# Unit stores moved on SyncE's queue, and three of fourteen low-part subtractions of a change of expert moved from VectorE to GpSimd

## The chip, the cores and the metric

The kernel runs on one core of a Trainium2 chip, alone. The metric is the device time of one execution in microseconds (us). The core's engines each work through a queue of their own, in order: TensorE (PE in the profile; its weight loads are PEld), VectorE (DVE), ScalarE (ACT), GpSimd (POOL) and SyncE (SP), which here only issues DMA transfers. They wait for each other on semaphores.

## The reference

Attention with a sigmoid instead of a softmax, then a mixture of experts in which each token goes to one of eight experts, then a gated layer. Everything is float32, apart from the last layer's weights, which come as float64.

```python
scores = scale * np.matmul(q, k.transpose(0, 1, 3, 2)) - np.log(S)      # q, k, v: 4 x 12 x 448 x 64
x = np.matmul(1.0 / (1.0 + np.exp(-scores)), v)                         # to 1792 tokens x 768
...
expert_idx = np.argmax(xn @ en.T / tau, axis=1)                         # one expert of 8 for each token
for e in range(E):
    h = np.maximum(x[mask] @ w1[e], 0.0)                                # w1: 768 x 1024
    out[mask] = gate_w[mask, None] * (h @ w2[e])                        # w2: 1024 x 768
...
return (out @ w_a * (out @ w_b)) @ w_out                                # 768 x 1536, 1536 x 768
```

## The kernel before

**Split products.** TensorE multiplies in a short form of float32 (fp32r in the rows). To keep the reference's precision each operand is split into a high part, a cast on ScalarE, and a low part, the operand minus its high part, a subtraction on VectorE. `split` (L787 the cast, L788 the subtraction) does both. Three products, high by high, low by high and high by low, are added up in PSUM.

**Attention** (0 to about 215 us) runs over 24 pairs of heads, `for i in range(NPR + 1)`. An iteration transposes the q and k of pair i+1, loads q and k of pair i+3 and v of pair i+2 (`load`, on SyncE's queue: q at L538, k at L531 and L533, v at L523 and L525), computes the scores of pair i with their sigmoids on ScalarE (L579, L584), and multiplies the sigmoids of pair i-1 by v (L601), with a turn back to token order two pairs behind (`x_tok`, copied out by VectorE at L617). `pump` runs pieces of the routing in between.

**Units.** In the background the float64 weights of the gated layer are turned into float32 in *units* of 128 x 384 numbers. `prep_load` brings one into `raw` (L182, L186, four buffers); VectorE cuts bits into `m` (L199, L201, two buffers); ScalarE converts the lower words (L203) and makes an absolute value in `ab` (L205, three buffers); GpSimd adds the two integer parts (L206); VectorE finishes the number in `ab` (`prep_finish`, L216); `prep_store` sends it to DRAM as `wm` (L229). `prep_tick` does these in the order store, finish, load, next unit; so `prep_store` sends what an earlier tick has finished.

**Mixture of experts** (210 to 540 us). Tokens are gathered by expert in blocks of 128, in two phases. A block transposes the gathered x (L783), splits it (`x_load`: high parts on ScalarE at L831, low parts on VectorE at L841), multiplies by w1 (`p1_half`: L911 to L913 in the first block, L891 after it), transposes the hidden values h (L962), splits them into hT (`h_split`, L970 and on VectorE L973), multiplies by w2 (`p2`, L1012), scales by the gate (`y_whole` or `y_half`, VectorE L1082 and L1090) and scatters the rows to DRAM from GpSimd's queue (L1104). GpSimd's queue also issues the gather of the block after next (`gather`, L812).

**Changes of expert.** When the next block belongs to another expert, that is known only at run time; the instructions of a change stand in branches (`when_new`). SyncE loads w1 and w2 into `r` (`load_w`, L799); then six parts of w1 (128 x 1024 each, kk = 0 to 5) and eight of w2 (128 x 768 each, kk = 0 to 7) are split by `split_w` into w1h, w1l, w2h and w2l. Within block b the order is: w1's kk 0 and 1 and then, after the next x, kk 2 to 5; at the end of the block w2's kk 0 to 3; in the block behind, w2's kk 4 and 5 after its first product with w1, and kk 6 and 7 after the second. The low parts of hT and of x stand between these on VectorE. In this run's trace the subtractions of a change begin at 280, 301, 352, 388, 408 and 463 us: two pairs that follow each other directly, and two single ones.

**First expert.** Its w1 is loaded and split during the last iterations of attention, one part for each step of the list `early_w`, which `first_expert` makes (an empty step and six splits).

**The gated layer** (540 to 1075 us) reads `wm`, splits it and multiplies; the change does not touch it.

What sets the order of the work is the order in which the program is written (the schedule is manual): each engine gets its instructions in that order. In the block behind a change that order is, in the code before:

```python
when_new(lambda: load_new(1), load)
p1(0, lambda: None)
...
if 0 < b < LIVE - 1:
    prep_store()
either(b, y_whole, y_half)
```

Of the kernel before, what the change touches and what calls it, by code (L numbers as in the profile page):

```python
# [9 lines left out]
F32 = mybir.dt.float32  # L10
# [14 lines left out]
def build(ctx: ExitStack, tc: tile.TileContext, q, k, v, emb, tau, w1, w2, wa, wb, wo, out, dbg=None, stop=None):  # L25
# [6 lines left out]
    nc = tc.nc  # L32
# [20 lines left out]
    LIVE = LIVE0 + -(-CAP[1] // P)  # L53
# [438 lines left out]
    def attention():  # L492
# [21 lines left out]
        def load(i, names):  # L514
            if i >= NPR:
                return
            b, hp = pairs[i]
            for nm in names:
                src = dict(q=q, k=k, v=v)[nm]
                sv = src[b, 2 * hp:2 * hp + 2].rearrange("h (p c) d -> p h c d", c=NCH)  # L520
                if nm == "v":
                    t = raw_p.tile([P, 2, NCH, D], F32, tag=nm, name=nm, bufs=4)
                    nc.sync.dma_start(out=t[:, :, :NCH - 1, :], in_=src[b, 2 * hp:2 * hp + 2, :KC].rearrange(  # L523
                        "h (p c) d -> p h (c d)", c=NCH - 1))
                    nc.sync.dma_start(out=t[half_of(i), :, NCH - 1, :],  # L525
                                      in_=src[b, 2 * hp:2 * hp + 2, KC:].rearrange("h p d -> p h d"))
                elif nm == "k":
                    t = raw_p.tile([P, NCH, 2, D], F32, tag=nm, name=nm, bufs=3)
                    dma = nc.scalar if i < 2 else nc.sync
                    for j in range(2):  # L530
                        dma.dma_start(out=t[:, :NCH - 1, j, :], in_=src[b, 2 * hp + j, :KC].rearrange(  # L531
                            "(p c) d -> p c d", c=NCH - 1))
                    nc.sync.dma_start(out=t[half_of(i), NCH - 1], in_=src[b, 2 * hp:2 * hp + 2, KC:].rearrange(  # L533
                        "h p d -> p h d"))
                else:
                    t = raw_p.tile([CP, NCH, 2, D], F32, tag=nm, name=nm, bufs=3)
                    for j in range(2):
                        nc.sync.dma_start(out=t[:, :, j, :], in_=sv[:, j])  # L538
                raw[i, nm] = t

        def tr_pair(i):

            if i == 1:
                pt = [p() for p in av_ps]
                parts = [(pt[s][:, :S], slice(s, s + 1)) for s in range(2)]
            else:
                both = ps_t.tile([P, 2, 512], F32, tag="pt", name="pt")
                pt = [both[:, s] for s in range(2)]
                parts = [(both[:, :, :S], slice(0, 2))]
            for s, nm in enumerate(("q", "k")):  # L550
                t = raw.pop((i, nm))
                for c in range(NCH):
                    cs, r = (slice(c * CP, (c + 1) * CP), slice(0, CP)) if nm == "q" else key_chunk(i, c)
                    nc.tensor.transpose(out=pt[s][:, cs], in_=t[r, c].rearrange("p h d -> p (h d)"), identity=ident[r, r])
            hi = qk_p.tile([P, 2, S], F32R, tag="qkh", name="qkh")
            lo = qk_p.tile([P, 2, S], F32R, tag="qkl", name="qkl")
            for src, ss in parts:
                h, l = (t[:, ss, :] if src.ndim == 3 else t[:, ss.start, :] for t in (hi, lo))
                nc.scalar.copy(out=h, in_=src)
                nc.vector.tensor_tensor(out=l, in0=src, in1=h.bitcast(F32), op=ALU.subtract)  # L560
            QK[i] = (hi, lo)
# [83 lines left out]
        for i in range(NPR + 1):  # L645
            if 0 < i and i + 1 < NPR:
                tr_pair(i + 1)
            load(i + 3, "qk")
            load(i + 2, "v")
            if i < NPR:  # L650
                score_half(i, 0)
            misc["ps"] = av_ps[i % 2]
            if i == NPR:
                one, turn = misc["ps"], [0]

                def either():
                    turn[0] ^= 1
                    return ps_s.tile([P, 2, 512], F32, tag="ps", name="pm2")[:, 0] if turn[0] else one()

                misc["ps"] = either  # L660
            pump((True,))
            if early_w is None and misc.get("flags0"):
                early_w = first_expert()
            if misc.get("tables0") and not misc.get("gathered"):
                gather(0)
                misc["gathered"] = True
            if early_w:
                early_w.pop(0)()
            if 1 <= i <= NPR:
                av_part(i - 1, 0)  # L670
            pump((True,))
            if i < NPR:
                score_half(i, 1)
            pump((LATE,))
            if i % 2 and i >= 2:
                x_tok(i - 2)
            if 1 <= i <= NPR:
                av_part(i - 1, 1)
            if i == NPR:
                both = ps_s.tile([P, 2, 512], F32, tag="ps", name="px0")  # L680
                x_load(0, [both[:, hf] for hf in range(2)])
                gather(1)
            if i >= 2:
                if i % 2 == 0:
                    x_tok(i - 2)
                b, hp = pairs[i - 2]
                if hp == NP - 1:
                    routed(b)
            if i < 3:
                prep_load(i)  # L690
            elif i < NPR:
                prep_tick(nc.sync)
                if i % 6 == 3 and i > 3:
                    prep_tick(nc.sync, 1)
            pump((END,))
# [101 lines left out]
    def load_w(which, expert, pair):  # L797
        t, src = (r1[pair], w1) if which == 1 else (r2[0][:, 2 * pair:2 * pair + 2, :], w2)
        nc.sync.dma_start(out=t, in_=src[expert, 2 * pair * P:2 * (pair + 1) * P, :].rearrange("(k p) c -> p k c", p=P))  # L799

    def split_w(which, kk, pool=None):
        hi, lo = (w1h, w1l) if which == 1 else (w2_t["h"], w2_t["l"])
        t = r1[kk // 2][:, kk % 2, :] if which == 1 else r2[0][:, kk, :]
        split(hi[kk], lo[kk], t, hi[kk].bitcast(F32))

    def gather(b):
        if b >= NBLK:
# [173 lines left out]
    def moe(r2_p):  # L981
# [8 lines left out]
        def block1(b, chg, was_new, load, e_load, live):  # L990
# [47 lines left out]

            if b > 0:
                when_new(lambda: load_new(1), load)  # L1040
                p1(0, lambda: None)
                when_new(lambda: split_new(2, KF // 2, KF - 2), was_new)
                tick()

                def rest():
                    when_new(lambda: split_new(2, KF - 2, KF), was_new)

                p1(1, rest)
                tick()
                if b < LIVE - 1:  # L1050
                    prep_tick()
                when_new(lambda: load_new(2), load)
# [37 lines left out]
                    nc.vector.scalar_tensor_tensor(out=yo[:PH], in0=yp[hf][PH:, :HD], scalar=gt[:PH], in1=yo[:PH],  # L1090
                                                   op0=ALU.mult, op1=ALU.add)

            if 0 < b < LIVE - 1:
                prep_store()
            either(b, y_whole, y_half)
            if live is not None:
                tc.mark_branch_hint_location(f"live{b + 1}", live, [ET.Activation, ET.DVE])
# [8 lines left out]

        for i in range(2, KF // 2):
            load_w(2, e_of[0], i)

        def block(b, was_new=None):  # L1110
            nx = b + 1
# [253 lines left out]
```

## Time and profile before

| | |
|---|---|
| time, median of 3 runs | 1075.32 us (1074.67 to 1077.29) |
| profiled execution: its own time | 1076.83 us |
| profiled execution: span from first to last instruction | 1074.9 us |
| mean granted clock of TensorE, as a share of its higher level | 0.997 |
| TensorE busy | 1049.5 us, 98% |
| VectorE busy | 592.3 us, 55% |
| ScalarE busy | 510.4 us, 47% |
| GpSimd busy | 154.2 us, 14% |
| TensorE's largest wait, for the first q at the start | 6.0 us |

The profile is of one execution; its own time is 1.5 us above the median of the runs. Busy shares are means over three stages that differ: VectorE is busy for 97% of the stretch from 280 to 320 us, and for 46% of the gated layer (246.8 of 535 us). A line of the timeline gives an instruction's start, its duration, the engine, the code's line and operation, the tile that it writes and those that it reads. Several equal instructions in a row stand on one line (x4) with the time from the start of the first to the end of the last.

### The profile page before, as it was taken

How to read it: one execution, taken by the hardware profiler on the slowest of the kernel's cores; microseconds unless marked ns; L12 is line 12 of the kernel's file. 1: busy time of each engine (PE TensorE's matmuls, PEld its weight loads, DVE VectorE, ACT ScalarE, POOL GpSimd, SP SyncE). 2: the span in 40 equal slices, each digit the busy share in tenths (PEclk: the TensorE clock that was granted, in tenths of full speed). 3: DMA queues.
4: the chain of work that ended last, by engine and by line, in shares of the span. 5: the costliest groups of instructions: out<-in, count | busy, mean ns of one | idle time of the engine just before them, and what ended most of it. 6: DMA issues, size and time to landing. Idle time of an engine off the chain costs nothing. (4 is left out here: it accounts for less than half of the span.)

```text
span 1074.9 us, 17443 instructions
## 1 busy us (share of the span) xinstructions
PE 1049.5 (98%) x5916; PEld 848.5 (79%) x5916; DVE 592.3 (55%) x1061; ACT 510.4 (47%) x803; POOL 154.2 (14%) x222
## 2 busy tenths in 40 slices
PE   7999999999999999999999999999999999999998
PEld 4554555488878977998978888888888888888997
DVE  2566698868793869372256786333333333333553
ACT  5777676543673777262155554333323322332542
POOL 2031221423222222221102222000000000000000
PEclk9999999999999999999999999999999999999999
DMA  6687769648589778822184644292220272210820
GB/s 161 170 207 200 186 175 260 197 146 292 174 307 331 253 262 305 317 86 101 47 279 176 221 132 145 105 361 109 88 88 1 107 289 89 89 45 1 350 105 30
DMA packets 118051, 187.84 MB, mean 175 GB/s; under 512 B 53928, under 2 KB 89000, under 8 KB 113072
## 3 DMA queue, kind: packets, MB, share of 16 engines
q1 hardware_dynamic: 113296, 171.10, 47.5%
q0 software_dynamic: 3040, 14.94, 3.9%
q8 instruction: 56, 0.92, 0.3%
q10 hardware_dynamic: 1600, 0.39, 0.2%
q14 instruction: 59, 0.48, 0.1%
HBM read 154.17 MB, written 32.24 MB: 173 GB/s over the span
## 5 line engine op out<-in xcount | busy, mean ns | idle before, releaser
L1229 PE MATMUL ab<-yh,whi 128*128 128x512 f32 (+1 forms) x576 | 209.3, 363 | 0.4 <-DVE yl L788 0.4
L1230 PE MATMUL ab<-yl,whi 128*128 128x512 f32 (+1 forms) x576 | 209.3, 363 | 0.2 <-DVE yl L788 0.2
L1231 PE MATMUL ab<-yh,wlo 128*128 128x512 f32 (+1 forms) x576 | 209.0, 363 | 0.0
L206 POOL TENSOR_TENSOR m<-m,raw 128x384 int32<-128x384 int32 x72 | 75.9, 1054 | 353.8 <-DVE m L201 193.4
L1231 PEld LDWEIGHTS ab<-yh,wlo 128*128 128x128 f32 x576 | 108.8, 189 | 17.3 <-DVE wlo L788 0.3
L1229 PEld LDWEIGHTS ab<-yh,whi 128*128 128x128 f32 x576 | 108.8, 189 | 16.3 <-ACT whi L787 0.5
L1230 PEld LDWEIGHTS ab<-yl,whi 128*128 128x128 f32 x576 | 108.8, 189 | 16.2 <-DVE yl L788 0.9
L1262 PE MATMUL o<-whi,gh 128*128 128x512 f32 x336 | 114.7, 341 | 0.0
L1263 PE MATMUL o<-whi,gl 128*128 128x512 f32 x336 | 113.7, 338 | 0.0
L1264 PE MATMUL o<-wlo,gh 128*128 128x512 f32 x336 | 113.0, 336 | 0.0
L1237 DVE TENSOR_TENSOR m<-ab,a 128x512 f32<-128x512 f32 (+1 forms) x48 | 30.0, 624 | 144.6 <-issue 126.5
L787 ACT CAST gh<-m 128x512 fp32r<-128x512 f32 (+1 forms) x48 | 27.2, 567 | 166.4 <-DVE m L1237 166.4
L584 ACT ACTIVATE a<-ps,bias_s 128x896 f32<-128x896 f32 x96 | 92.9, 1006 | 26.5 <-PE ps L579 25.8
L788 DVE TENSOR_TENSOR wlo<-r,whi 128x768 fp32r<-128x768 f32 x76 | 68.6, 954 | 57.3 <-ACT whi L787 57.3
L787 ACT CAST whi<-r 128x768 fp32r<-128x768 f32 x76 | 58.9, 833 | 54.6 <-PE o L1263 46.0
L601 PE MATMUL av<-a,v 128*64 128x448 f32 (+1 forms) x384 | 79.8, 571 | 2.0 <-DVE xtok L617 2.0
L788 DVE TENSOR_TENSOR wlo<-wx,whi 128x768 fp32r<-128x768 f32 x57 | 51.2, 954 | 44.0 <-ACT whi L787 44.0
L1262 PEld LDWEIGHTS o<-whi,gh 128*128 128x128 f32 x336 | 63.4, 189 | 8.2
L1263 PEld LDWEIGHTS o<-whi,gl 128*128 128x128 f32 x336 | 63.4, 189 | 7.5
L1264 PEld LDWEIGHTS o<-wlo,gh 128*128 128x128 f32 x336 | 63.1, 188 | 7.4
L973 DVE SCALAR_TENSOR_TENSOR hTl<-px,hTh 128x512 fp32r<-128x512 f32 x35 | 24.1, 689 | 73.2 <-ACTq L993 63.7
L787 ACT CAST whi<-wx 128x768 fp32r<-128x768 f32 x57 | 43.8, 832 | 40.7 <-PE o L1263 36.0
(271 smaller groups left out, 1847.6 us busy)
## 6 DMA issues: line engine op xcount, KB each, us to landing
r<-in_moe_w_dram SPq DMA_DIRECT2D x28, 768.0 KB, 14.6
wx<-wm SPq DMA_DIRECT2D x18, 1152.0 KB
r<-wm SPq DMA_DIRECT2D x17, 1152.0 KB, 5.6
r<-in_moe_w_dram SPq DMA_DIRECT2D x18, 1024.0 KB, 10.9
raw<-in_moe_w_a_dram SPq DMA_DIRECT2D x24, 384.0 KB, 3.7
raw<-in_moe_w_b_dram SPq DMA_DIRECT2D x24, 384.0 KB, 3.7
raw<-in_moe_w_out_dram SPq DMA_DIRECT2D x24, 384.0 KB, 3.9
wm<-ab SPq DMA_DIRECT2D x48, 192.0 KB, 2.6
```

The source lines that it names most:

```text
L206: nc.gpsimd.tensor_tensor(out=m, in0=m, in1=low, op=ALU.add)
L584: nc.scalar.activation(out=a[r], in_=ps[:n, :, :S], func=AF.Sigmoid, bias=bias_s[:n], scale=qscale)
L601: nc.tensor.matmul(av[w][j * D:(j + 1) * D, :S], lhsT=raw[w, "v"][r, j, c, :], rhs=a[r, j, :], start=first, stop=last)
L787: nc.scalar.copy(out=hi, in_=src)
L788: eng.tensor_tensor(out=lo, in0=src, in1=f32_hi, op=ALU.subtract)
L1229: nc.tensor.matmul(ps[:, :n], lhsT=hi[:, s, cs], rhs=yh[:, kk, :n], start=kk == 0, stop=False)
L1230: nc.tensor.matmul(ps[:, :n], lhsT=hi[:, s, cs], rhs=yl[:, kk, :n], start=False, stop=False)
L1231: nc.tensor.matmul(ps[:, :n], lhsT=lo[:, s, cs], rhs=yh[:, kk, :n], start=False, stop=kk == KD - 1)
L1237: nc.vector.tensor_tensor(out=m, in0=ps[:, :n], in1=a, op=ALU.mult)
L1262: nc.tensor.matmul(t[:, d0:d1], lhsT=gh[:, cs], rhs=hi[:, 2, d0:d1], start=first, stop=False)
L1263: nc.tensor.matmul(t[:, d0:d1], lhsT=gl[:, cs], rhs=hi[:, 2, d0:d1], start=False, stop=False)
L1264: nc.tensor.matmul(t[:, d0:d1], lhsT=gh[:, cs], rhs=lo[:, 2, d0:d1], start=False, stop=last)
```

## The change

Four edits. In attention, `prep_store` is called ahead of the loads of q, k and v in each iteration, besides its call in `prep_tick`. The step of `early_w` is taken ahead of the lines that make that list, so that each step comes an iteration later, and the last one behind the loop. In the mixture of experts, `prep_store` moves from the place ahead of y's scaling to the place behind w1's loads at the head of the block. And `split_w` gives the subtraction of w1's part kk = 3 and of w2's parts kk = 2 and 5 to GpSimd; this holds at each change of expert, and for w2's part 5 also once in the first block, where the first expert's w2 parts 4 to 7 are split.

```diff
--- before.py
+++ after.py
@@ -645,6 +645,7 @@
         for i in range(NPR + 1):
             if 0 < i and i + 1 < NPR:
                 tr_pair(i + 1)
+            prep_store()
             load(i + 3, "qk")
             load(i + 2, "v")
             if i < NPR:
@@ -658,14 +659,14 @@
                     return ps_s.tile([P, 2, 512], F32, tag="ps", name="pm2")[:, 0] if turn[0] else one()
 
                 misc["ps"] = either
+            if early_w:
+                early_w.pop(0)()
             pump((True,))
             if early_w is None and misc.get("flags0"):
                 early_w = first_expert()
             if misc.get("tables0") and not misc.get("gathered"):
                 gather(0)
                 misc["gathered"] = True
-            if early_w:
-                early_w.pop(0)()
             if 1 <= i <= NPR:
                 av_part(i - 1, 0)
             pump((True,))
@@ -798,10 +799,12 @@
         t, src = (r1[pair], w1) if which == 1 else (r2[0][:, 2 * pair:2 * pair + 2, :], w2)
         nc.sync.dma_start(out=t, in_=src[expert, 2 * pair * P:2 * (pair + 1) * P, :].rearrange("(k p) c -> p k c", p=P))
 
+    on_pool = {}
+
     def split_w(which, kk, pool=None):
         hi, lo = (w1h, w1l) if which == 1 else (w2_t["h"], w2_t["l"])
         t = r1[kk // 2][:, kk % 2, :] if which == 1 else r2[0][:, kk, :]
-        split(hi[kk], lo[kk], t, hi[kk].bitcast(F32))
+        split(hi[kk], lo[kk], t, hi[kk].bitcast(F32), nc.gpsimd if kk in on_pool.get(which, ()) else nc.vector)
 
     def gather(b):
         if b >= NBLK:
@@ -1038,6 +1041,8 @@
 
             if b > 0:
                 when_new(lambda: load_new(1), load)
+                if b < LIVE:
+                    prep_store()
                 p1(0, lambda: None)
                 when_new(lambda: split_new(2, KF // 2, KF - 2), was_new)
                 tick()
@@ -1090,8 +1095,6 @@
                     nc.vector.scalar_tensor_tensor(out=yo[:PH], in0=yp[hf][PH:, :HD], scalar=gt[:PH], in1=yo[:PH],
                                                    op0=ALU.mult, op1=ALU.add)
 
-            if 0 < b < LIVE - 1:
-                prep_store()
             either(b, y_whole, y_half)
             if live is not None:
                 tc.mark_branch_hint_location(f"live{b + 1}", live, [ET.Activation, ET.DVE])
@@ -1106,6 +1109,8 @@
 
         for i in range(2, KF // 2):
             load_w(2, e_of[0], i)
+
+        on_pool.update({1: (3,), 2: (2, 5)})
 
         def block(b, was_new=None):
             nx = b + 1
```

Lines of the code behind the first edit move: the subtraction of L788 is L789 in the changed kernel, the gather of L812 is L815, y's scatter of L1104 is L1107.

SyncE's queue in attention, in the iteration that starts near 93 us: q, k, v and raw are loads into SBUF tiles of those names, wm is the store of a finished unit. Before:

```order
L186 DMA raw<-in_moe_w_out_dram 128x768
L538 DMA q<-in_q_dram 112x4x64 x2
L531 DMA k<-in_k_dram 128x3x64 x2
L533 DMA k<-in_k_dram 64x2x64
L523 DMA v<-in_v_dram 128x2x192
L525 DMA v<-in_v_dram 64x2x64
L229 DMA wm_69<-ab 128x384 x2
L182 DMA raw<-in_moe_w_a_dram 128x3x256
```

In the changed kernel:

```order
L186 DMA raw<-in_moe_w_out_dram 128x768
L229 DMA wm_69<-ab 128x384 x2
L538 DMA q<-in_q_dram 112x4x64 x2
L531 DMA k<-in_k_dram 128x3x64 x2
L533 DMA k<-in_k_dram 64x2x64
L523 DMA v<-in_v_dram 128x2x192
L525 DMA v<-in_v_dram 64x2x64
L182 DMA raw<-in_moe_w_a_dram 128x3x256
```

The two stores stand ahead of the five lines of loads instead of behind them.

GpSimd's queue in a block of the mixture of experts, from x's transposes to y's scatter; xg is the gathered x, m a unit's integer part, the branches are those of `when_new` and of the block's other conditions. Before:

```order
L823 UNCONDITIONAL_BRANCH
L993 COMPARE_AND_BRANCH
L993 UNCONDITIONAL_BRANCH x2
L812 DMA xg<-xs,idx_100 128x768
L876 UNCONDITIONAL_BRANCH
L206 TENSOR_TENSOR m<-m,raw 128x384
...
L1104 DMA ys<-y,idy_102 5376x768
```

In the changed kernel, and on to the first branch behind the scatter:

```order
L789 TENSOR_TENSOR w1l_131<-r_1_2831,w1h_125 128x1024
L996 UNCONDITIONAL_BRANCH x3
L815 DMA xg<-xs,idx_100 128x768
L879 UNCONDITIONAL_BRANCH
L206 TENSOR_TENSOR m<-m,raw 128x384
...
L789 TENSOR_TENSOR w2l_2825<-r_2946,w2h_2817 128x768
L996 UNCONDITIONAL_BRANCH x2
L1107 DMA ys<-y,idy_102 5376x768
...
L789 TENSOR_TENSOR w2l_2828<-r_2946,w2h_2820 128x768
```

At a change, w1's part stands ahead of the gather and of the unit's addition, w2's kk 2 between that addition and the scatter, and w2's kk 5 behind the scatter.

VectorE's queue in the same block, the low parts of w1's kk 2 to 5 and what follows. Before:

```order
L788 TENSOR_TENSOR w1l_130<-r_1_2830,w1h_124 128x1024
L788 TENSOR_TENSOR w1l_131<-r_1_2830,w1h_125 128x1024
L788 TENSOR_TENSOR w1l_132<-r_2_2831,w1h_126 128x1024
L788 TENSOR_TENSOR w1l_133<-r_2_2831,w1h_127 128x1024
L993 UNCONDITIONAL_BRANCH x2
L216 SCALAR_TENSOR_TENSOR ab<-ab,m 128x384
```

In the changed kernel:

```order
L789 TENSOR_TENSOR w1l_130<-r_1_2831,w1h_124 128x1024
L789 TENSOR_TENSOR w1l_132<-r_2_2832,w1h_126 128x1024
L789 TENSOR_TENSOR w1l_133<-r_2_2832,w1h_127 128x1024
L996 UNCONDITIONAL_BRANCH x3
L216 SCALAR_TENSOR_TENSOR ab<-ab,m 128x384
```

The second of the four subtractions is gone from this queue; the unit's finish follows the third.

## Rows read from the trace of the kernel before

**Rows 1.** The page's first part: busy time, share of the span, instructions.

```profile
PE 1049.5 (98%) x5916; PEld 848.5 (79%) x5916; DVE 592.3 (55%) x1061; ACT 510.4 (47%) x803; POOL 154.2 (14%) x222
```

**Rows 2.** TensorE's waits: engine, line, releaser: us in total, times, longest us.

```profile
PE av L601 <- DVE xtok L617: 2.0, 2, 1.8
PE ps L579 <- ACT a L584: 1.6, 1, 1.6
```

**Rows 3.** Stretches in attention: us, busy PE, PEld, DVE, ACT, POOL, PEclk, DMA, GB/s.

```profile
100.00:105.00 5.00, 3.40 (x24) 1.83 (x23) 1.93 (x4) 2.81 (x4) 1.01 (x1) 1.00 0.93 262
105.00:110.00 5.00, 4.97 (x27) 2.44 (x24) 1.47 (x3) 3.23 (x5) 0.00 (x0) 0.66 0.79 208
205.00:210.00 5.00, 5.00 (x23) 2.12 (x22) 4.54 (x15) 0.26 (x1) 2.07 (x2) 0.67 0.00 0
```

**Rows 4.** Two stretches of the same view where changes of expert follow each other.

```profile
280.00:300.00 20.00, 20.00 (x113) 18.08 (x111) 19.43 (x26) 18.20 (x28) 5.54 (x4) 1.00 0.53 179
300.00:320.00 20.00, 17.69 (x89) 14.41 (x89) 19.26 (x25) 15.10 (x24) 5.26 (x4) 1.00 0.89 335
```

**Rows 5.** ScalarE's timeline: start us, us, instruction, in brackets idle time before it.

```profile
102.19 0.56 ACT L205 ACTIVATE ab<-raw 128x384 f32<-128x384 bf16 x1 [3.91 <-DMA wm<-ab]
```

**Rows 6.** SyncE's queue on the timeline; last, how long `ab`'s stores took to land.

```profile
93.60 2.57 SPq L538 DMA_DIRECT2D q<-in_q_dram  x2
99.59 1.01 SPq L229 DMA_DIRECT2D wm<-ab  x2
...
DMA to landing us min/median/max: 2.5/3.6/4.7
```

**Rows 7.** VectorE's timeline ahead of those stores.

```profile
92.48 1.02 DVE L216 SCALAR_TENSOR_TENSOR ab<-ab,m 128x384 f32<-128x384 f32 x2
```

**Rows 8.** Timelines of ScalarE and TensorE around the first expert's sixth step.

```profile
203.91 1.04 ACT L787 CAST w1h<-r 128x1024 fp32r<-128x1024 f32 x1
210.84 0.48 ACT L831 CAST xh<-px 128x384 fp32r<-128x384 f32 x1 [0.62 <-DVE xl L860]
...
214.64 0.39 PE L912 MATMUL p<-w1l,xh 128*128 128x512 f32 x1
```

**Rows 9.** VectorE's timeline at the change at 352 us.

```profile
355.98 4.62 DVE L788 TENSOR_TENSOR w1l<-r,w1h 128x1024 fp32r<-128x1024 f32 x4
363.71 5.30 DVE L788 TENSOR_TENSOR w2l<-r,w2h 128x768 fp32r<-128x768 f32 x6
368.93 0.68 DVE L973 SCALAR_TENSOR_TENSOR hTl<-px,hTh 128x512 fp32r<-128x512 f32 x1
```

**Rows 10.** GpSimd's elementwise forms: one line's durations (min/median/max), one group of lines.

```profile
L206 POOL TENSOR_TENSOR m<-m,raw x48: 1009/1021/2062, 38.4 to 449.7; 128x384 int32<-128x384 int32 x48
...
L114 POOL TENSOR_TENSOR fold<-ident 128x64 f32<-128x64 f32 x2 | 0.6, 320 | 0.0
```

**Rows 11.** Timelines of VectorE and GpSimd where their instructions meet.

```profile
300.82 1.83 DVE L788 TENSOR_TENSOR w1l<-r,w1h 128x1024 fp32r<-128x1024 f32 x1
...
300.55 1.02 POOL L206 TENSOR_TENSOR m<-m,raw 128x384 int32<-128x384 int32 x1 [6.91 <-DVE m L201]
...
205.33 1.21 DVE L788 TENSOR_TENSOR w1l<-r,w1h 128x1024 fp32r<-128x1024 f32 x1
...
205.35 2.06 POOL L206 TENSOR_TENSOR m<-m,raw 128x384 int32<-128x384 int32 x1 [5.65 <-ACT w1h L787]
```

**Rows 12.** Timelines of TensorE and GpSimd after the change at 352 us.

```profile
361.13 1.52 PE L891 MATMUL p<-w1l,xh 128*128 128x512 f32 x6
370.49 1.55 PE L1012 MATMUL p<-w2h,hTl 128*128 128x384 f32 x8
...
362.18 1.03 POOL L206 TENSOR_TENSOR m<-m,raw 128x384 int32<-128x384 int32 x1 [6.18 <-DVE m L201]
```

**Rows 13.** Timelines of VectorE and TensorE at the last change.

```profile
477.12 0.68 DVE L973 SCALAR_TENSOR_TENSOR hTl<-px,hTh 128x512 fp32r<-128x512 f32 x1
...
480.79 1.55 PE L1012 MATMUL p<-w2h,hTl 128*128 128x384 f32 x8
```

## The prediction

> **What bounds the kernel now.** The page's first part comes first: TensorE is busy 98% of the span [rows 1], so a change counts by what it takes from, or adds to, TensorE's 25 us of idle time, and by the clock granted to TensorE. Next, the list of what TensorE waited for [rows 2]. Once the first loads are there, two single waits stand out, both in attention: 1.6 us for ScalarE's sigmoids and 1.8 us for a copy of VectorE. Behind each of them the table of stretches shows a granted clock of 0.66 and 0.67 for about 5 us, where it is 1.00 elsewhere [rows 3]: each wait costs its own length and then some 5 x 0.34 = 1.7 us more.
>
> Then the mixture of experts. TensorE hardly waits there, but at a change of expert VectorE is not idle either: where two changes follow each other it is busy 38.7 of 40 us [rows 4]. So the second question is how much VectorE may be late before TensorE notices.
>
> **Stores ahead of q, k, v.** The wait of 1.6 us, just before 105 us, has its origin in ScalarE's queue: from 98.3 us on its activation into `ab` stands still for 3.91 us until a unit's store has landed, and the cast of the next pair's q and k stands behind it [rows 5]. The two stores left at 99.59 us, behind q, k and v that SyncE had begun to issue at 93.60 us [rows 6], although VectorE had finished what they store by 93.5 us [rows 7]. With the stores ahead of q, k, v they leave at about 93.6 us and land within 2.5 to 4.7 us as such stores do [rows 6], at the latest at 98.3 us, when ScalarE asks. The stall goes, and with it TensorE's 1.6 us and the 1.7 us of clock: **-3.3 us**. Bounds: 0, if another wait takes that place, and -6.8 if the second wait (1.8 us and its 1.7 us of clock) goes as well; I count nothing for that one, because in the new order a low part of w1 still stands ahead of that copy on VectorE. That q, k, v leave about 1 us later I cost at nothing: they are issued two pairs ahead of the transposes that read them; the price without that cover would be up to 1 us for each pair.
>
> **First expert's low parts.** Moving the pop ahead of the two lines that make the list shifts all six steps by one iteration; the sixth falls behind the loop, after x's high parts. Its cast starts at 211.3 us, when ScalarE is through with x [rows 8], takes 1.04 us as the fifth part's did [rows 8], and the subtraction 1.15 to 1.21 us [rows 9, 11]: ready at 213.6 us, a microsecond before TensorE reads it at 214.64 [rows 8]. I cost it at nothing; if VectorE's queue delays it by 2 us, it costs 1 us.
>
> **Unit stores behind w1's loads.** SyncE reaches w1's loads without first waiting for VectorE's unit, so they leave some microseconds earlier where two changes follow each other. There ScalarE's casts waited for weights, but VectorE, whose subtractions follow these casts, was busy all along [rows 4]. So I count nothing for it; the most it could return is TensorE's idle time in such a stretch, 20.00 - 17.69 = 2.3 us [rows 4]. In exchange a store now waits until w1's loads have found their buffers free, and `ab` comes back later to ScalarE, whose casts of weights stand behind the activation that waits for it. `ab` has three buffers and a block makes at most two units, so I cost that at nothing; without the cover it would be a stall like the one in attention, 1.6 us of TensorE.
>
> **Three low parts on GpSimd.** This is the term that decides. VectorE gives up one of w1 (4.62 / 4 = 1.15 us) and two of w2 (5.30 / 6 = 0.88 us each) at a change [rows 9]. No row shows GpSimd subtracting weights. Its addition of 384 columns takes 1.02 us and one of 64 columns 0.32 us [rows 10]; the line through both gives 2.42 us for 1024 columns and 1.86 us for 768. Bounds: VectorE's own 1.15 and 0.88 below, and in proportion to the 384 columns above, 2.72 and 2.04.
>
> Does VectorE go on working meanwhile? At 300.82 us a subtraction of w1 takes 1.83 us, where another takes 1.21; GpSimd's addition runs until 301.57, and from there the subtraction needs those 1.1 to 1.2 us [rows 11]. The reverse is there too: at 205.35 us GpSimd's addition takes 2.06 us, because VectorE began such a subtraction 0.02 us earlier [rows 11]. So an elementwise instruction of GpSimd and a subtraction of VectorE from two SBUF tiles run one after the other, not side by side.
>
> The Trainium skill says the same as a rule (SBUF — State Buffer, "Who interferes with whom"): a VectorE instruction with two SBUF inputs and a GpSimd instruction that reads SBUF share a port, and the second to come waits for the whole of the first. It speaks against this change, and the rows above agree; by it the sum is the one below, without it the first rival's.
>
> So each moved part costs VectorE's chain GpSimd's time less its own: 2.42 - 1.15 = 1.27 us for w1, 1.86 - 0.88 = 0.98 us for each of w2. The single change at 352 us shows what TensorE feels. VectorE finishes w1's last low part at 360.60 us; TensorE reads it as the last of six that start at 361.13, at 362.3 [rows 9, 12]: 1.27 us late is still in time. GpSimd's addition for a unit follows this and now ends near 364.5 us instead of 363.21 [rows 12]; w2's 3rd part goes straight behind it, and VectorE's subtractions stand until it is done. The 6th comes behind the scatter of y and stops VectorE once more, before hT's low part. That is ready at 369.61 us now and read at 370.49 [rows 9, 12]: 0.88 us of slack against 1.27 + 2 x 0.98 = 3.23 us. TensorE loses 2.35 us.
>
> There are six changes. Two pairs follow each other directly (the first at 280 and 301 us [rows 4, 11]); with VectorE full, nothing is caught up between the two: 2 x 3.23 - 0.88 = 5.6 us a pair. The one at 352 us costs 2.35. The last has no units beside it: GpSimd's part of w2 falls beside y's scaling, and hT's low part is ready at 477.80 us, 3.0 us before it is read [rows 13], against 3.2 us: nothing. The gather that now stands behind w1's part on GpSimd fetches what is read a block later, some 20 us on where two changes follow each other (280 and 301 us): its 2.4 us cost nothing; without that cover they would come on top at each change. Sum: 2.35 + 2 x 5.6 = **+13.5 us**, in pieces of about 1 us, shorter than the waits behind which the clock fell, so I add nothing for the clock.
>
> By the figure of the Trainium skill (GPSIMD Engine Reference, "3.1 Elementwise — side-by-side cycle accounting": 4497 ns for an addition of 2048 columns) the two sizes would be about 2.25 and 1.69 us, an estimate, and the sum +11 instead of +13.5 us. No run here shows it yet.
>
> **Sum.** -3.3 + 13.5 = +10.2 us. The profiled execution took 1076.83 us, which becomes 1087.0; the median of the runs is 1075.32, 1.5 us lower, so I forecast **1085.5 us**.
>
> **Rivals.** First, the other side: GpSimd's subtraction of fp32 lets VectorE's run beside it, where the integer addition did not. VectorE is then 2.9 us earlier at each change, and TensorE's waits in the two pairs go, 2 x 2.3 us [rows 4]; with attention's 3.3 that is -7.9: 1067.4 us. What decides is whether a subtraction of VectorE beside one of GpSimd keeps its 1.21 us; against it stand the two collisions of [rows 11], for it only that none of them is fp32.
> Second, the instructions do exclude each other, but GpSimd's turns fall mostly where VectorE waits or reads PSUM, or w1's earlier loads move the pairs: a third of 13.5 remains, +4.5 - 3.3 = +1.2: 1076.5 us. Against it: VectorE has 1.3 us free in 40 [rows 4].
> Third, it is dearer: GpSimd needs 2.72 and 2.04 us, 3.89 us a change, so 3.0 + 2 x 6.9 = 16.8; and the waits grow long enough to lower the clock twice, 3.4 us: +20.2 - 3.3 = 1092.2 us; without the clock 1088.8, which is also what comes if attention gives nothing.
>
> **How the numbers follow.** The forecast (1079 to 1088.5) 0.50; the first rival 0.17; the second 0.15; the third 0.18. A measurement of this kernel tells about 0.3% from no change, 1072.1 to 1078.5 us. Faster: the first rival and a little, 0.18. Same: most of the second, 0.14. Slower: 0.68. The range reaches down into the second rival and up to the third, 1074 to 1092, and leaves out the first and the ends.
>
> **What would show it.** Right: GpSimd's three rows at a change near 2.4 and 1.9 us; subtractions of VectorE of 2 to 3.5 us that end 0.9 to 1.2 us after GpSimd's; TensorE waiting for hT's and w2's low parts on VectorE, about 1 us at a time; no wait of ScalarE for a unit's store in attention, and no clock of 0.66 near 105 us. Wrong: VectorE's subtractions all at 1.21 and 0.95 us (the first rival), or stretched ones without new waits of TensorE (the second).

## The result, and the profile after

The changed kernel takes 1087.13 us (median of 6 runs, 1086.57 to 1089.2) where the kernel before takes 1075.68: a ratio of 1.011, 95% interval 1.0098 to 1.0123, or 11.5 us more. The forecast was 1085.5 us. The profiled execution took 1087.26 us, with a span of 1085.5; its span is 10.6 us longer than that of before.

The changed kernel's page, first part, and the list of what TensorE waited for (us in total, times, longest us):

```profile
PE 1052.4 (97%) x5916; PEld 852.1 (78%) x5916; DVE 606.1 (56%) x1042; ACT 510.1 (47%) x803; POOL 188.8 (17%) x241
```

```profile
PE p L1015 <- DVE w2l L789: 6.7, 6, 1.7
...
PE p L894 <- DVE xl L844: 4.7, 2, 2.4
PE p L1015 <- DVEq L996: 3.5, 5, 1.8
PE av L601 <- DVE xtok L617: 1.9, 2, 1.7
```

Against [rows 1]: VectorE made 19 instructions fewer and was busy 13.8 us longer. It didn't get more work; its instructions stood still inside. That is seen in the durations of the changes' subtractions (count, then ns min/median/max), before:

```profile
L788 DVE TENSOR_TENSOR w2l<-r,w2h x48: 944/951/959, 291.8 to 478.6; 128x768 fp32r<-128x768 f32 x48
L788 DVE TENSOR_TENSOR w1l<-r,w1h x36: 1207/1215/1833, 280.6 to 469.7; 128x1024 fp32r<-128x1024 f32 x36
```

In the changed kernel, with GpSimd's own:

```profile
L789 DVE TENSOR_TENSOR w2l<-r,w2h x32: 943/946/2800, 293.9 to 484.9; 128x768 fp32r<-128x768 f32 x32
L789 DVE TENSOR_TENSOR w1l<-r,w1h x30: 1211/1218/3421, 280.3 to 481.2; 128x1024 fp32r<-128x1024 f32 x30
L789 POOL TENSOR_TENSOR w2l<-r,w2h x11: 1840/1847/1868, 291.7 to 482.3; 128x768 fp32r<-128x768 f32 x11
L789 POOL TENSOR_TENSOR w1l<-r,w1h x6: 2396/2582/3030, 284.4 to 477.6; 128x1024 fp32r<-128x1024 f32 x6
```

Against [rows 2]: the wait for ScalarE's sigmoids (L579 on L584, 1.6 us) is gone, the one for `xtok` is still there, and, apart from the wait for the first q, three entries head the list, all of them VectorE's: low parts of w2 and low parts of x, which are new, and, as "DVEq", VectorE's queue that comes late to a branch (1.3 us in 4 waits before).

The table of stretches, for the changed kernel (columns as in [rows 3]):

```profile
100.00:105.00 5.00, 5.00 (x36) 2.36 (x32) 1.83 (x3) 3.96 (x5) 1.02 (x1) 1.00 0.72 202
105.00:110.00 5.00, 5.00 (x40) 3.23 (x39) 4.04 (x8) 4.32 (x6) 1.02 (x1) 1.00 0.89 222
200.00:206.00 6.00, 6.00 (x31) 2.82 (x30) 5.31 (x17) 1.67 (x3) 1.14 (x2) 0.72 0.33 117
238.00:242.00 4.00, 4.00 (x19) 4.00 (x18) 2.40 (x9) 0.75 (x2) 1.01 (x1) 0.57 0.15 53
310.00:314.00 4.00, 4.00 (x12) 3.15 (x11) 3.97 (x7) 0.89 (x2) 0.00 (x0) 0.57 0.29 99
422.00:426.00 4.00, 3.78 (x10) 3.02 (x11) 4.00 (x6) 2.40 (x4) 0.55 (x1) 0.61 0.46 129
```

The clock of 0.66 behind 105 us [rows 3] is 1.00 now. The one behind 200 us has stayed, and three new ones have come, at 238, 310 and 422 us. Each takes about 1.7 us of TensorE's time: 6 x 0.28 for the first, 4 x 0.43 for the second and third; the fourth lasts beyond the end of its stretch.

Where the time went is seen when the same matmul of TensorE is looked up in two traces. In times of the kernel before, 197 to 253 us holds the end of attention and the experts' first block, 275 to 345 the first pair of changes, 345 to 391 the single one, 391 to 454 the second pair. The table gives the lead (-) or lag (+) in us against the trace of before, for the changed kernel and for the experiments below, from one profile each. At 90 us, ahead of the first effect, they lie between -0.4 and +0.1:

| kernel | 105 | 197 | 253 | 275 | 345 | 391 | 454 | end |
|---|---|---|---|---|---|---|---|---|
| changed kernel | -1.8 | -4.1 | -0.7 | -0.3 | +3.5 | +5.6 | +10.5 | +10.6 |
| a_no_pool | -1.6 | -2.5 | -2.4 | -1.6 | -2.7 | -2.7 | -3.4 | -3.3 |
| b_pool_only | -0.6 | -2.2 | +1.0 | +1.1 | +4.9 | +6.9 | +11.8 | +11.9 |
| c_pool_from_change | -1.7 | -3.9 | -2.2 | -1.9 | +3.3 | +6.8 | +13.0 | +13.1 |
| d_pool_short | -2.0 | -4.3 | -4.1 | -3.1 | -6.5 | -6.5 | -9.9 | -9.8 |
| k_first_block_only | -1.7 | -3.9 | -3.1 | -2.7 | -3.8 | -3.9 | -4.5 | -4.2 |
| e_att_store | -1.7 | -3.5 | -4.0 | -4.0 | -4.0 | -4.0 | -4.0 | -4.0 |
| g_moe_store | -0.3 | -1.8 | -1.8 | -1.7 | -3.4 | -3.4 | -4.1 | -4.0 |
| l_two_stores | -2.1 | -3.9 | -4.3 | -3.7 | -4.9 | -4.9 | -5.5 | -5.2 |

In the changed kernel attention gains, the first block gives 3.4 us of it back, the two pairs lose 3.8 and 4.9 us and the single change 2.1; the last change loses nothing.

**The single change**, where [rows 9] and [rows 12] stand for before. GpSimd's, VectorE's and TensorE's timelines of the changed kernel:

```profile
360.38 2.60 POOL L789 TENSOR_TENSOR w1l<-r,w1h 128x1024 fp32r<-128x1024 f32 x1 [5.23 <-ACT w1h L788]
363.13 1.78 POOL L815 DMA_INDIRECT xg<-xs,idx  x1 [0.16 <-PE p L894]
366.76 1.03 POOL L206 TENSOR_TENSOR m<-m,raw 128x384 int32<-128x384 int32 x1 [1.85 <-ACT w2h L788]
367.75 1.84 POOL L789 TENSOR_TENSOR w2l<-r,w2h 128x768 fp32r<-128x768 f32 x1
369.75 1.12 POOL L1107 DMA_INDIRECT ys<-y,idy  x1 [0.16 <-PE p L894]
370.89 1.86 POOL L789 TENSOR_TENSOR w2l<-r,w2h 128x768 fp32r<-128x768 f32 x1
```

```profile
361.29 3.90 DVE L789 TENSOR_TENSOR w1l<-r,w1h 128x1024 fp32r<-128x1024 f32 x2 [0.59 <-ACT w1h L788]
...
366.45 1.14 DVE L1087 TENSOR_SCALAR y<-p,slots 128x384 f32<-128x384 f32 x2
367.83 2.18 DVE L216 SCALAR_TENSOR_TENSOR ab<-ab,m 128x384 f32<-128x384 f32 x1 [0.24 <-POOL m L206]
369.93 5.38 DVE L789 TENSOR_TENSOR w2l<-r,w2h 128x768 fp32r<-128x768 f32 x4
```

```profile
371.39 0.52 PE L1015 MATMUL p<-w2h,hTh 128*128 128x384 f32 x2
373.62 0.62 PE L1015 MATMUL p<-w2l,hTh 128*128 128x384 f32 x2 [1.72 <-DVE w2l L789]
```

To read there: `ab`'s finish on VectorE, 0.51 us in [rows 7], takes 2.18 us at 367.83; GpSimd's w2 part began at 367.75 and ends at 369.59, 0.42 us before it. The four subtractions of w2 take 5.38 us in place of 4 x 0.88: GpSimd's second part runs in the middle of them. TensorE feels that at once, at the low part of w2's second row block, 1.72 us. y's scaling at 366.45, which reads PSUM, lies beside GpSimd's addition (366.76 to 367.79) and takes its usual time (1.14 us for two, as in the kernel before at 311.31 us). On this last point the trace agrees with the Trainium skill (SBUF — State Buffer, "Who interferes with whom"): outside VectorE's two-port modes an instruction with at most one SBUF input doesn't contend with GpSimd.

**The second change of a pair** shows something else. TensorE, VectorE and GpSimd of the changed kernel:

```profile
422.22 2.40 PE L894 MATMUL p<-w1h,xh 128*128 128x512 f32 x6 [2.36 <-DVE xl L844]
```

```profile
416.52 5.18 DVE L789 TENSOR_TENSOR w1l<-r,w1h 128x1024 fp32r<-128x1024 f32 x2
421.62 1.01 DVE L844 TENSOR_TENSOR xl<-px,xh 128x384 fp32r<-128x384 f32 x2
```

```profile
418.22 2.40 POOL L789 TENSOR_TENSOR w1l<-r,w1h 128x1024 fp32r<-128x1024 f32 x1 [0.95 <-ACT w1h L788]
```

In program order w1's kk 3 comes after the next x. But GpSimd's queue is empty and VectorE's is not: GpSimd takes kk 3 at 418.22 us, just ahead of VectorE's kk 1, which then stands until 420.62. Behind it stands x's low part, and for that TensorE waits 2.36 us; the clock falls behind this wait. The same happens in the first pair (2 waits, 4.7 us in the list above).

The fall of the clock adds little to the loss of the first pair, since TensorE, slower for a while, then waits less for VectorE. The changed kernel's next wait of the first pair, and the same wait in b_pool_only, whose clock doesn't fall in that pair:

```profile
320.98 0.62 PE L1015 MATMUL p<-w2l,hTh 128*128 128x384 f32 x2 [0.62 <-DVE w2l L789]
```

```profile
322.36 0.62 PE L1014 MATMUL p<-w2l,hTh 128*128 128x384 f32 x2 [1.71 <-DVE w2l L788]
```

Both kernels lose 3.8 us in the first pair (table).

### The profile page after: what moved, and what is told of

Read it like the earlier page. It is cut to its first block, busy times and chain, and to the rows that moved or that the text cites. A ratio compares the mean times of both kernels' runs of the same rounds, so it can differ in the third digit from the quotient of the medians.

```text
span 1085.5 us, 17566 instructions
## 1 busy us (share of the span) xinstructions
PE 1052.4 (97%) x5916; PEld 852.1 (78%) x5916; DVE 606.1 (56%) x1042; ACT 510.1 (47%) x803; POOL 188.8 (17%) x241
## 4 chain that ended last, share of the span: by engine, by line
PE 52%; DVE 1%; issue 0%; ACT 0%; POOL 0%; ACTq 0%; POOLq 0%
PE ab L1235 11%; PE ab L1236 11%; PE ab L1234 11%; PE o L1267 6%; PE o L1268 5%; PE o L1269 5%; PE p L1015 2%; PE p L894 2%; PE ab L784 0%; DVE yl L789 0%; PE px L965 0%; PE px L784 0%; DVE wlo L789 0%; PE px L963 0%; DVE y L1087 0%
## 5 line engine op out<-in xcount | busy, mean ns | idle before, releaser
L584 ACT ACTIVATE a<-ps,bias_s 128x896 f32<-128x896 f32 x96 | 92.8, 1005 | 32.4 <-PE ps L579 31.8
L788 ACT CAST gh<-m 128x512 fp32r<-128x512 f32 (+1 forms) x48 | 27.2, 567 | 167.2 <-DVE m L1242 167.2
L789 DVE TENSOR_TENSOR wlo<-r,whi 128x768 fp32r<-128x768 f32 x76 | 68.6, 955 | 57.1 <-ACT whi L788 57.1
L788 ACT CAST whi<-r 128x768 fp32r<-128x768 f32 x76 | 59.0, 833 | 54.3 <-PE o L1268 46.1
L789 DVE TENSOR_TENSOR wlo<-wx,whi 128x768 fp32r<-128x768 f32 x57 | 51.2, 954 | 43.3 <-ACT whi L788 43.3
L1015 PE MATMUL p<-w2h,hTl 128*128 128x384 f32 x288 | 60.1, 343 | 3.5 <-DVEq L996 3.5
```

The lines of the kernel that those rows point to most:

```text
L584: nc.scalar.activation(out=a[r], in_=ps[:n, :, :S], func=AF.Sigmoid, bias=bias_s[:n], scale=qscale)
L788: nc.scalar.copy(out=hi, in_=src)
L789: eng.tensor_tensor(out=lo, in0=src, in1=f32_hi, op=ALU.subtract)
L1015: nc.tensor.matmul(yp[hf][:, :HD], lhsT=l[:, kk, :], rhs=wv[kk][:, hf * HD:(hf + 1) * HD], start=kk == 0 and i == 0 and len(parts) == 2, s ...
```

## The experiments

Each was timed beside the kernel before; ratios are to that, with 95% intervals. One per cent is 10.8 us.

**a_no_pool.** The changed kernel without GpSimd's parts:

```diff
-        on_pool.update({1: (3,), 2: (2, 5)})
```

> The changed kernel without the three parts on GpSimd: only the stores and the first expert's steps are moved. My theory (the loss is GpSimd's three subtractions, which keep VectorE waiting, and the moved stores gain in attention alone): 1075.7 - 4 = 1071.7 us; the -4 is what the changed kernel had gained by 201 us, 4.4 us, less the 0.44 us by which its first load came earlier. Rival one (the stores behind w1's loads cost or gain in the experts, too): off by over 1.5 us from that, and the difference arises between 280 and 430 us. Rival two (the loss comes from the moved stores and not from GpSimd): near 1083 to 1087 us.

1072.05 us, ratio 0.9962 (0.9947 to 0.9977). The loss is GpSimd's parts: 1.011 - 0.9962 makes 15.9 us. The time is within 0.4 us of my theory's. But the gain is not attention's alone: part of it arises in the pairs (table: -1.1 and -0.7 us), so rival one is right about the place, not about the size.

**b_pool_only.** The kernel before, with those lines of the diff alone that hold `on_pool`:

```diff
+    on_pool = {}
...
+        split(hi[kk], lo[kk], t, hi[kk].bitcast(F32), nc.gpsimd if kk in on_pool.get(which, ()) else nc.vector)
...
+        on_pool.update({1: (3,), 2: (2, 5)})
```

> The kernel before with the three parts on GpSimd and nothing else. My theory: the changed kernel lost 4.2 us in the first block, 3.9 and 5.2 us in the two pairs of changes and 1.9 us in the single one, all through GpSimd, and 0 in the last; so 1075.7 + 15.2 = 1090.9 us, and in attention the two waits of the kernel before are still there. Rival (the earlier loads of w1 brought the changes of expert closer and added to the loss): the pairs cost clearly less than 9.1 us, 1086 us or below; or, if the earlier loads had helped, more than 1093 us.

1090.21 us, ratio 1.0145 (1.0123 to 1.0167), +15.6 us. By the table 3.2 us arise from 197 to 253 us, 3.8 and 4.9 in the pairs, 2.0 in the single change: the changed kernel's pattern, with no help from the stores.

**c_pool_from_change.** The first block's part goes back to VectorE:

```diff
                 split_new(2, 4, KF)
+                on_pool.update({1: (3,), 2: (2, 5)})
...
-        on_pool.update({1: (3,), 2: (2, 5)})
```

> The changed kernel, but the first block's w2 part 5 goes back to VectorE; the changes of expert stay as they are. My theory (that one part delays the gather and the routing's small operations behind it on GpSimd by 1.7 us, TensorE waits 1.8 us for hT's low part and then loses about as much by the lower clock): 1087.1 - 4 = 1083.1 us, with no wait of TensorE near 237 us and a clock of 1.00 from 238 to 242 us. Rival (the first block's wait has to do with its shifted first expert's steps or with the stores, not with this part): 1086 to 1088 us, the wait still there.

1089.73 us, ratio 1.013 (1.0109 to 1.015): not faster. The wait near 237 us is gone, but 1.7 us are lost from 197 to 253 us all the same, because the low clock behind 200 us lasts twice as long here (0.50 from 204 to 206 us, where the changed kernel has 0.90). And the table shows that the changes cost more: 5.2, 3.5 and 6.2 us in place of 3.8, 2.1 and 4.9. For the single change the reason is seen on TensorE's timeline of this kernel, at the place shown above for the changed one:

```profile
371.21 0.51 PE L1015 MATMUL p<-w2h,hTh 128*128 128x384 f32 x2
373.45 0.62 PE L1015 MATMUL p<-w2l,hTh 128*128 128x384 f32 x2 [1.72 <-DVE w2l L789]
373.90 0.87 PE L965 MATMUL px<-ident,h 128*128 128x128 f32 x4
374.42 0.99 PE L1015 MATMUL p<-w2h,hTh 128*128 128x384 f32 x2
```

In the changed kernel the two lines that follow the same wait of 1.72 us read:

```profile
374.08 0.60 PE L965 MATMUL px<-ident,h 128*128 128x128 f32 x4
374.43 0.60 PE L1015 MATMUL p<-w2h,hTh 128*128 128x384 f32 x2
```

Same instructions, same wait, but 0.99 us for two matmuls in place of 0.60: here the clock fell (0.57 from 374 to 378 us), there it did not (1.00). That is 1.4 us (3.5 - 2.1). In the pairs the clock falls once in either kernel, but here at the last wait of the pair (1.73 us, until 319.4, and 1.74 us, until 435.7), with no later wait to take up the loss. So the time of such a kernel depends on which of its waits the clock falls behind, and a wait removed early in the kernel can be outweighed by that. My expectation failed, and this run doesn't say what the first block costs.

**d_pool_short.** As c, with shorter subtractions on GpSimd:

```diff
+        if kk in on_pool.get(which, ()):
+            cs = slice(0, 64)
+            nc.scalar.copy(out=hi[kk], in_=t)
+            nc.gpsimd.tensor_tensor(out=lo[kk][:, cs], in0=t[:, cs], in1=hi[kk].bitcast(F32)[:, cs], op=ALU.subtract)
...
```

> As the kernel before this one, but each of GpSimd's three subtractions at a change takes 64 columns instead of 1024 or 768, so most of these three low parts is left out; queues, waits and VectorE's relief are the same. My theory (the price is the time for which GpSimd's instruction keeps VectorE's from starting): VectorE gives up 2.9 us at each change and stands for some 0.3 us three times, so the pairs lose nothing and gain up to 2.3 us each: 1067 to 1072 us. Rival (the price is the new waits and branches in the queues, GpSimd's starting late or the gather behind it, not the length of its instructions): above 1077 us.

1067.71 us, ratio 0.9921 (0.9906 to 0.9937): 22 us less than c, with the same queues and waits. The length of GpSimd's instructions is the price. Against a_no_pool it is 4.4 us less: that is what VectorE's relief is worth in itself, and by the table it arises in the pairs (3.4 us gained in each, in place of 1.1 and 0.7). In the stretch of the first pair this kernel has no wait at all and VectorE is free for 5.3 us (columns as in [rows 4]):

```profile
280.00:320.00 40.00, 40.00 (x217) 36.22 (x216) 34.69 (x50) 32.17 (x52) 14.89 (x16) 1.00 0.78 271
```

**j_unread.** As c, but TensorE does not read GpSimd's results:

```diff
+            run_over(xh, w1l[:3] + w1l[2:3] + w1l[4:], last=True)
...
+                            wk = wv[kk - 1 if b and wv is w2l and kk in (2, 5) else kk]
```

> As the run in which GpSimd has its three parts from the first change of expert on, and GpSimd writes them in full, but TensorE reads the neighbouring low parts in their place from the second block on, so the product leaves these three low parts out and counts their neighbours' twice: no instruction of TensorE waits for GpSimd's results. My theory (GpSimd's instructions keep VectorE's from starting): the time stays where it was, 1087 to 1091 us, and VectorE's subtractions of 2.8 us are all there. Rival (TensorE waits for GpSimd's own late results): near 1070 us.

1085.72 us, ratio 1.0093 (1.008 to 1.0107), a little below the range that I gave. Nothing of TensorE waits for GpSimd here, yet 14.1 us of c's 18.1 (both against a_no_pool) are there. VectorE's subtractions as grouped for that run (ns min/median/max):

```profile
L789 DVE TENSOR_TENSOR w2l<-r,w2h x34: 941/947/2789, 291.2 to 483.9; 128x768 fp32r<-128x768 f32 x34
L789 DVE TENSOR_TENSOR w1l<-r,w1h x30: 1210/1218/3431, 277.6 to 478.5; 128x1024 fp32r<-128x1024 f32 x30
```

The stretched ones are there, up to 2.79 and 3.43 us. The remaining 4 us fit the clock: c's profile has two falls more among the changes (three against one), and its low clock behind 200 us lasts twice as long; that is read from two profiles, not shown.

**k_first_block_only.** The kernel a with the first block's part alone on GpSimd:

```diff
+        on_pool.update({2: (5,)})
...
                 split_new(2, 4, KF)
+                on_pool.clear()
```

> The run without GpSimd's parts (1072.1 us), but with the first block's w2 part 5 on GpSimd, and none at the changes. My theory (this one part delays the gather and the routing's small operations on GpSimd by 1.7 us; TensorE waits 1.8 us near 237 us and loses 1.7 us by the clock): 1075.5 us. Rival (it costs nothing by itself, as the run in which it alone was taken back did not become faster): 1072 us, without the wait.

1073.91 us, ratio 0.9975 (0.9965 to 0.9985), 1.4 us above a_no_pool, with intervals that overlap: between my theory and the rival. In the profile TensorE waits 0.84 us at 236.4 us, without a fall of the clock; in the changed kernel it is 1.79 us, with one. GpSimd's queue shows a reason. The changed kernel's timeline, then this one's:

```profile
222.51 1.88 POOL L789 TENSOR_TENSOR w2l<-r,w2h 128x768 fp32r<-128x768 f32 x1 [15.59 <-PE p L1015]
225.25 1.67 POOL L815 DMA_INDIRECT xg<-xs,idx  x1 [0.86 <-POOLq L996]
```

```profile
222.52 1.90 POOL L789 TENSOR_TENSOR w2l<-r,w2h 128x768 fp32r<-128x768 f32 x1 [15.48 <-ACT w2h L788]
224.56 1.51 POOL L815 DMA_INDIRECT xg<-xs,idx  x1
```

In the changed kernel GpSimd stands 0.86 us at the branch around w1's part (L996), and the gather starts 0.69 us later. Behind the gather stand the routing's small operations of phase 2, then VectorE's chain that turns them into y and hT's low part, and TensorE at its end. That the later gather makes up the whole difference of the two waits (0.95 us) fits, but is not shown by a run of its own.

**e_att_store, f_early_w, g_moe_store, l_two_stores.** Each is the kernel before with some of the other hunks of the diff: the first alone, the second alone, the moved store of the experts alone, and the first with the moved store. As an example, what l changes:

```diff
+            prep_store()
             load(i + 3, "qk")
...
                 when_new(lambda: load_new(1), load)
+                if b < LIVE:
+                    prep_store()
...
-            if 0 < b < LIVE - 1:
-                prep_store()
             either(b, y_whole, y_half)
```

> The kernel before with the first edit alone: a unit's stores ahead of q, k and v. My theory (this edit takes away the wait of 1.6 us near 104 us and the 1.7 us by the clock behind it, and is the whole gain of the run without GpSimd's parts, 3.2 us): 1075.3 - 3.3 = 1072.0 us. Rival (part of the gain comes from the first expert's steps or from the stores behind w1's loads): 1073 to 1075 us, and one of those two edits alone would then be below 1075.

1072.7 us, ratio 0.9969 (0.9957 to 0.998): -3.3 us, as my theory had it.

> The kernel before with the second edit alone: each of the first expert's steps an iteration later. My theory: 1075.3 us, within 1 us; the wait of 1.7 us near 200 us is in all runs so far, with these steps earlier or later. Rival (the sixth step, behind the loop, is late for TensorE): up to 2 us more, with a wait of TensorE for w1's low part near 214 us.

1077.56 us, ratio 1.0019 (1.001 to 1.0027): +2.0 us. In the profile TensorE waits 1.2 us at 210.9 us for x's low part on VectorE, where the first expert's fifth step (206.5 us) and the routing stand ahead of it; there is no wait for w1's sixth low part. Since g, which has the steps where they were, also waits there (2.0 us), I can't say that the later steps cause this wait; the cause of the 2 us stays open.

> The kernel before with the third edit alone: the experts' unit stores behind w1's loads. My theory (the earlier loads take away ScalarE's wait of 1.6 us for w1 in the second change of each pair, which in the run without GpSimd's parts gave back 1.1 and 0.7 us): 1075.3 - 1.8 = 1073.5 us. Rival (that gain needs the other edits; VectorE is the bound there as the prediction had it): 1075.3 us, within 1 us.

1074.51 us, ratio 0.9981 (0.9971 to 0.9991): -2.0 us, my theory. ScalarE's wait for w1 at the second change of a pair shows it; its timeline without the moved stores (e_att_store), then with them (a_no_pool):

```profile
300.43 2.00 ACT L788 CAST w1h<-r 128x1024 fp32r<-128x1024 f32 x2 [1.58 <-DMA r<-in_moe_w_dram]
```

```profile
299.30 3.91 ACT L788 CAST w1h<-r 128x1024 fp32r<-128x1024 f32 x4
```

Two casts that waited 1.58 us for their weights now follow the others at once; in g itself the four take 3.91 us from 299.12 us on. What TensorE gains by it is its own waits for ScalarE, whose copies of h and high parts of hT stand behind such casts in its queue. Before, all of them in the pairs:

```profile
PE p L1012 <- ACT hTh L970: 1.5, 2, 0.7
...
PE px L962 <- ACT h L914: 1.3, 3, 0.8
```

In g neither is left.

> The two moves of the stores together, without the first expert's later steps and without GpSimd's parts. My theory (3.3 us in attention and 1.8 us in the pairs add up, and the first expert's later steps had only cost): 1070.2 us, the fastest kernel that computes all. Rival (the two gains do not add up, or the later steps were needed for one of them): 1072 us or more, no faster than the run without GpSimd's parts.

1071.2 us, ratio 0.9948 (0.9935 to 0.9962): the two gains add up to 5.6 us. Apart from d_pool_short it is the fastest kernel here; a_no_pool, with the first expert's later steps besides, lies 1.5 us above it, in line with what f costs, though the two intervals overlap.

**h_pool_w1, i_pool_w2.** As c, with one kind of part each:

```diff
+                on_pool.update({1: (3,)})
```

```diff
+                on_pool.update({2: (2, 5)})
```

> The changed kernel with w1's part alone on GpSimd, from the first change of expert on. My theory (VectorE loses some 1.3 us net at each change; a slack of 0.9 us covers most of it at the single one, and at each pair 2 x 1.3 - 0.9 = 1.7 us are left): 1072 + 0.4 + 3.4 = 1075.8 us, or 1.7 us more for each fall of the clock. Rival (one moved part is hidden, only w2's cost): 1072 to 1073 us.

1078.23 us, ratio 1.0018 (1.0007 to 1.0028): 6.0 us above a_no_pool, where I expected 3.8, or 5.5 with one fall of the clock. Its profile has one among the changes, a low clock behind 200 us that lasts twice as long as in the changed kernel, and the two waits for x's low part, 4.7 us.

> The changed kernel with w2's two parts alone on GpSimd, from the first change of expert on. My theory (VectorE loses 2 x 1 us net at each change: 1.1 us at the single one, 3.0 us at each pair): 1072 + 7.1 = 1079.1 us, or 1.7 us more for each fall of the clock. Rival (w1's part is the one that costs, since its instruction is the longest): under 1075 us.

1080.53 us, ratio 1.0043 (1.0028 to 1.0059): 8.7 us above a_no_pool, expected 7.1. No fall of the clock among the changes; TensorE's list shows 7.3 us for w2's low parts in 7 waits.

## Why the prediction was right, and where its steps were off

The forecast of +10.2 us met +11.5, by terms that were partly wrong.

**Attention, -3.3 us.** Right: e_att_store measures -3.3. The stores leave SyncE at 93.24 us in the changed kernel, ScalarE's activation into `ab` waits 0.38 us at 98.57 in place of 3.91 [rows 5], and the wait and its fall of the clock are gone. The second wait stayed, as assumed. The size, though, owes something to chance: b, f and g, which keep the old order there, wait 1.1 to 1.4 us for the sigmoids and the clock doesn't fall.

**First expert, 0.** Right in its reason (no wait for the sixth low part), wrong in its sum: f_early_w costs 2.0 us.

**Stores behind w1's loads, 0, at most -2.3.** Mis-sized: -2.0. The step "VectorE was busy all along" [rows 4] followed the late casts to VectorE alone. TensorE also waits for ScalarE directly, for h and hT's high parts behind those casts, 2.8 us before and nothing in g.

**GpSimd's three parts, +13.5.** The mechanism was right and is shown: d and j separate the length of GpSimd's instructions from their results and their queue. The durations were right: 2.40 us (at 418.22, the shortest of six; the median is 2.58) and 1.84 to 1.87 us where 2.42 and 1.86 were read off a line through two other forms [rows 10]. The estimate from the Trainium skill's figure (GPSIMD Engine Reference, "3.1 Elementwise — side-by-side cycle accounting"), 2.25 and 1.69 us, was lower than this trace shows. The term measured 15.6 us (b against before) and 15.9 (changed kernel against a). By its parts, in the changed kernel's profile and with the clock's share in them:
- the single change, forecast 2.35: 2.1, but TensorE waits for w2's low part, not for hT's. That w2's 6th stops VectorE "once more" was foreseen; that it does so ahead of the second of w2's own low parts was not.
- the pairs, forecast 5.6 each: 3.8 and 4.9. The two waits of 2.4 us for x's low part come from GpSimd taking w1's kk 3 ahead of VectorE's kk 1; I had placed w1's collision behind x.
- the last change, forecast 0: 0.
- the first block, not in the sum at all: 3.4 us in the profile. I had costed the gather behind GpSimd's part at nothing with the cover of a block; in the first block it is not the gather but the routing's chain behind it that is late. By itself this part costs 1.4 us (k); the rest came with the further branch and the fall of the clock.
- the clock, forecast 0: the step "pieces of about 1 us, shorter than the waits behind which the clock fell" failed. The waits became 1.7 to 2.4 us, and the clock fell behind three of them. What that adds is 1.7 us in the first block, and little in the pairs, where the next wait shrinks (to 0.62 and 0.71 us). Nor does a short wait keep the clock up: it fell behind 0.7 and 0.8 us in a_no_pool, at 536 us.

So the first block, which was missed, makes up for pairs that were forecast 2.5 us too dear, and the stores' -2.0 for the steps' +2.0: that the total came so near is in part luck.

**The rivals.** The first, ports free, was wrong in its condition but right in its price: with GpSimd's instructions made short, 1067.7 us against 1067.4. The second, GpSimd's turns in VectorE's idle time or w1's earlier loads, found neither: VectorE's subtractions stood, and b, without those loads, loses 15.6 us where 4.5 were its price. The third's lowering of the clock was real, without its dearer instructions.

## What to carry to other kernels

Before work moves from VectorE to GpSimd, look for two elementwise instructions of these engines that already meet in the trace, VectorE's with both inputs in SBUF: if the one is longer by what is left of the other, a moved instruction doesn't free VectorE, it stops it for GpSimd's longer time (here 2.4 us for 1.15). A free engine also takes its instruction earlier than the program order suggests, so it can stop something that stands ahead of it in the text. And the moves of stores, worth 5.6 us, were hidden in the same change: measure edits apart before the whole is dropped.

## What the runs showed of the hardware that was not expected

After the same wait of TensorE, 1.72 us at the same instruction, the granted clock fell in one kernel (two matmuls 0.99 us) and not in the other (0.60 us). In g_moe_store it fell behind none of the waits of 1.3, 1.4 and 2.0 us in attention and behind it, and its mean clock over the span is 1.000. And two waits of 0.7 and 0.8 us at the start of the gated layer stand in the changed kernel (at 548.7 and 549.9 us, clock 1.00 behind them) and in a_no_pool (at 534.8 and 536.0 us), where the clock is 0.57 from 536 to 540 us. A fall takes about 1.7 us of TensorE's time; it costs less where TensorE waits again soon after. Behind which waits it comes I can't tell from these runs.
